# Pooled attention and a max-of-two feed-forward on one core: the first K load in two parts, and matmuls on a tile of ones at the start

## The chip, the core and the metric

The kernel runs on one core of one Trainium2 chip. The metric is the device time of one execution in microseconds; the number to compare is the median of several runs. Besides, one execution is recorded by the hardware profiler, and every duration below comes from that one.

The engines are named as in the profile: PE is TensorE's matmul and PEld its weight load, DVE is VectorE, ACT ScalarE, POOL GpSimd, SP SyncE. SPq is SP's queue of DMA issues.

## The reference

```python
def _attn_ref(q, k, v):                       # 8 x 8 heads, 1152 tokens, 64 wide
    scale = 1.0 / np.sqrt(D)
    q_pool = q.reshape(B, H, S // 2, 2, D).mean(axis=3)
    scores = scale * np.matmul(q_pool, k.transpose(0, 1, 3, 2))
    scores = scores - np.max(scores, axis=-1, keepdims=True)
    attn = np.exp(scores)
    attn = attn / (np.sum(attn, axis=-1, keepdims=True) + 1e-09)
    return np.matmul(attn, v).astype(np.float32)

def _moe_ref(x, w1, w2, w_out):               # x: 4608 x 512; w1, w2: 512 x 1024; w_out: 1024 x 512
    g = np.maximum(x @ w1, x @ w2)
    return (g @ w_out).astype(np.float32)
```

The heads' outputs, side by side, are the rows x. Inputs and output are float32.

## The kernel before, in words

**Pairs, groups, blocks.** Two heads of one batch are a pair; there are 32 pairs. For each pair, K (1152 x 64 for two heads) is loaded as kraw (128 partitions, 2 heads, 9 tiles of 64), cast to bf16 (kbf) and transposed to kT, 9 tiles of 128 columns. Q is loaded as qraw, two neighbouring rows are added (qp), and it is transposed to qpT (576 columns). The scores of a pair are a strip of 9 x 576 columns for each of the two heads; the strips of all pairs are laid end to end and cut into groups of 512 columns. For a group, PE computes both heads' scores into one of three PSUM tiles (sps0, sps1, sps2, in turn; line 548), and ACT takes the exponential of 128 x 1024 elements into et (line 555). When a pair's groups are done, PE multiplies et with V (lines 459 and 471), DVE normalizes (lines 481 to 491), and the result is transposed to xT. The feed-forward part follows, interleaved with later pairs.

**The beginning.** Pair 0 is handled in parts. Q comes in two loads (line 304), of 4 and 5 of 9 row groups: QA = 256 columns first, the other 320 later. Pair 0's strip is laid out accordingly: first all 9 tiles against the first 256 columns, then all 9 against the other 320. A group therefore has two K tiles at first: group 1 tiles 0 and 1, group 2 tiles 2 and 3, and so on; the fifth group has tile 8 with the first Q part and tile 0 with the second. K0 = (0, 2, 4, 9) cuts the first K's cast: tiles 0 to 1 and 2 to 3 by ACT (line 329), 4 to 8 by POOL (line 332). All three wait for the one load of kraw0 (line 296). PE transposes each part (line 428), DVE copies it to kT (line 435). Q's parts are added by DVE (line 346), transposed by PE (line 395), copied by DVE (line 402).

**What else runs early.** SP issues the loads in the order: first Q part, K0, second Q part, a quarter of w2 (line 626, into a free part of xT), Q1, K1, V0, and then more weights, Q, K and V. DVE turns each w2 quarter to bf16 (line 633) and each w_out quarter (line 637); PE transposes w2 (line 651), DVE copies (line 657); the product w2 with w_out is made later (line 667). POOL casts K1, K2, ... (line 320), adds Q2, Q3, ... (line 353), and casts V (line 359).

**Order.** The program builds a plan: each op names what it reads and writes, its engine and a cost; a planner emits ops by these modelled times. Then reorder() puts PE's and DVE's ops into an order written out by hand as strings. A letter of pe_order is the next op of that lane: "S" a score op, a digit an op that writes that PSUM bank. An op whose first written key begins with "s" is in lane S. In dve_order, "Q" is what belongs to no bank (the early adds), "W" the weight conversions, a digit the bank read. solve() puts in the semaphore waits; each engine runs its list strictly in order. On DVE the order at the start is: add of Q's first part, its copy, two kT copies, add of Q's second part, kT copy of tiles 4 to 8, conversion of w2's first quarter (633), copy of Q's second part (402).

## Time and profile before

| | us |
|---|---|
| median of 3 runs | 366.93 (366.34 to 367.17) |
| the profiled execution, its time | 366.77 |
| its span, first to last instruction | 365.1 |
| PE busy | 353.3 (97%), 5797 matmuls |
| ACT busy | 315.2 (86%) |
| DVE busy | 242.0 (66%) |
| POOL busy | 125.5 (34%) |
| DMA | 84.70 MB, mean 232 GB/s |

A row of the profile gives the line, the engine, the operation and the tiles (out<-in, without buffer numbers), how many, and then busy time, mean length and the idle time in front. A timeline row has start and length in us. Engines work side by side, so busy times don't add up to the span. A matmul's length includes its run through the array; neighbours overlap, so the pitch of a row of matmuls is shorter than the length of one.

### The profile page before, as it was taken

To read this page: it belongs to the slowest core of one execution; us is meant where nothing else is said; L and a number is where in the kernel's file an instruction comes from. 1 tells how busy PE (TensorE), PEld (TensorE's weight loads), DVE (VectorE), ACT (ScalarE), POOL (GpSimd) and SP (SyncE) were. 2 spreads that over 40 slices of the span, in tenths; PEclk is the share of its full clock that TensorE was granted. 3 is DMA by queue.
4 is the path that set the end of the run, shared out by engine and by line. 5 is a ranking of instruction groups with operands and counts; after the bars stand their busy time and mean duration, and the time that the engine had idled before them with its cause. 6 is when DMAs were issued, how large, how long until landed. Compare 5 with 4: busy or idle time off the path is not lost.

```text
span 365.1 us, 13058 instructions
## 1 busy us (share of the span) xinstructions
PE 353.3 (97%) x5797; PEld 217.3 (60%) x5797; DVE 242.0 (66%) x522; ACT 315.2 (86%) x356; POOL 125.5 (34%) x111
## 2 busy tenths in 40 slices
PE   3899999999999999999999999999999999999996
PEld 1466655665466656556666655656676664656563
DVE  3587478878688767785886955886778565533321
ACT  4999999999999999999999999999999999971221
POOL 1258984325453441461253421443434220000000
PEclk9899999999999999999999999999999999999999
DMA  7999997997999999997969999969999540422124
GB/s 284 407 394 399 397 297 247 239 275 210 287 324 254 272 294 327 265 341 196 322 137 232 254 264 306 239 144 262 343 283 198 75 107 20 75 18 59 41 76 115
DMA packets 77400, 84.70 MB, mean 232 GB/s; under 512 B 49952, under 2 KB 50208, under 8 KB 77344
## 3 DMA queue, kind: packets, MB, share of 16 engines
q1 hardware_dynamic: 76624, 82.82, 85.4%
q8 instruction: 45, 0.74, 0.9%
q10 hardware_dynamic: 720, 1.05, 0.8%
q14 instruction: 11, 0.09, 0.1%
HBM read 62.91 MB, written 9.44 MB: 198 GB/s over the span
## 4 chain that ended last, share of the span: by engine, by line
PE 93%; ACT 3%; DMA 1%; ACTq 1%; DVE 1%; issue 0%; SPq 0%; DVEq 0%
PE sps L548 22%; PE fb L789 13%; PE sps L459 11%; PE sps L756 10%; PE fb L459 10%; PE sps L789 7%; PE sps L822 5%; PE fb L756 5%; ACT et L555 3%; PE fb L667 2%; PE sps L471 2%; PE fb L471 2%; DMA kraw<-in_k_dram 1%; PE sps L729 1%; PE fb L428 1%; ACTq L693 1%
## 5 line engine op out<-in xcount | busy, mean ns | idle before, releaser
L555 ACT ACTIVATE et<-sps 128x1024 bf16<-128x1024 f32 (+1 forms) x336 | 306.4, 1006 | 15.5 <-PE sps L548 14.0
L548 PE MATMUL sps<-qpT,kT 64*128 64x256 bf16 (+7 forms) x1162 | 121.3, 288 | 1.4 <-ACT et L555 1.2
L413 DVE STREAM_TRANSPOSE qpT<-qp 32x288 bf16<-32x288 bf16 x216 | 101.4, 470 | 6.8 <-PE sps L548 2.4
L548 PEld LDWEIGHTS sps<-qpT,kT 64*128 64x128 bf16 x1162 | 46.8, 94 | 50.9 <-ACT et L555 16.4
L353 POOL TENSOR_TENSOR qp<-qraw 128x576 bf16<-128x576 f32 x30 | 42.2, 1406 | 76.3 <-DVE qpT L413 62.5
L359 POOL TENSOR_SCALAR vE<-vraw 128x1152 bf16<-128x1152 f32 x32 | 37.0, 1156 | 83.8 <-PE sps L459 52.0
L756 PE MATMUL sps<-xT,wd 64*128 64x512 bf16 (+3 forms) x448 | 52.6, 327 | 0.0
L789 PE MATMUL fb<-wo,stage 64*128 64x512 bf16 x288 | 43.5, 376 | 0.0
L459 PE MATMUL sps<-vE,et 128*128 128x65 bf16 x1224 | 43.4, 193 | 0.0
L765 DVE TENSOR_SCALAR stage<-sps 128x1024 bf16<-128x1024 f32 (+3 forms) x28 | 27.3, 974 | 23.6 <-PE sps L756 23.4
L459 PEld LDWEIGHTS sps<-vE,et 128*128 128x128 bf16 x1224 | 39.2, 97 | 5.9 <-issue 4.6
L459 PE MATMUL fb<-vE,et 128*128 128x65 bf16 x1080 | 39.4, 193 | 0.0
L459 PEld LDWEIGHTS fb<-vE,et 128*128 128x128 bf16 x1080 | 34.8, 97 | 7.5 <-issue 6.7
L320 POOL TENSOR_SCALAR kbf<-kraw 128x1152 bf16<-128x1152 f32 x31 | 35.7, 1151 | 9.5 <-DMA kraw<-in_k_dram 7.7
L756 PEld LDWEIGHTS sps<-xT,wd 64*128 64x128 bf16 x448 | 19.9, 94 | 14.7 <-DVE xT L615 1.2
L756 PE MATMUL fb<-xT,wd 64*128 64x512 bf16 (+3 forms) x192 | 23.2, 332 | 0.0
L789 PE MATMUL sps<-wo,stage 64*128 64x512 bf16 x160 | 23.2, 376 | 0.0
L789 PE MATMUL fb<-w,xT 64*128 64x512 bf16 x144 | 21.3, 376 | 0.0
L789 PEld LDWEIGHTS fb<-wo,stage 64*128 64x128 bf16 x288 | 13.4, 94 | 8.6
L765 DVE TENSOR_SCALAR stage<-fb 128x1024 bf16<-128x1024 f32 (+3 forms) x12 | 12.0, 1002 | 9.4 <-PE fb L756 9.2
L822 PE MATMUL sps<-wo,stage 128*128 128x512 bf16 (+2 forms) x64 | 15.7, 352 | 0.0
L481 DVE RECIPROCAL rc<-sps 128x5 f32<-128x5 f32 (+1 forms) x34 | 6.3, 187 | 14.0 <-PE sps L459 13.6
(71 smaller groups left out, 270.2 us busy)
## 6 DMA issues: line engine op xcount, KB each, us to landing
kraw<-in_k_dram SPq DMA_DIRECT2D x32, 576.0 KB, 7.1
vraw<-in_v_dram SPq DMA_DIRECT2D x32, 576.0 KB, 7.5
qraw<-in_q_dram SPq DMA_DIRECT2D x31, 576.0 KB, 5.8
out_dram<-stage SPq DMA_DIRECT2D x19, 256.0 KB, 7.3
out_dram<-stage SPq DMA_DIRECT2D x25, 128.0 KB, 3.3
xT<-in_moe_w_dram SPq DMA_DIRECT2D x4, 512.0 KB, 10.5
stage<-in_moe_w_out_dram SPq DMA_DIRECT2D x4, 512.0 KB, 13.9
stage<-in_moe_w_dram SPq DMA_DIRECT2D x4, 512.0 KB, 14.2
```

What stands on the lines that cost most here:

```text
L320: op("POOL", lambda g: g.tensor_scalar(kbf[s][:, :, :, :].rearrange("p t h d -> p h t d"), kraw[r][:, :, :, :], 1.0, 1.0, ALU.mult, ALU.mu ...
L353: op("POOL", lambda g: g.tensor_tensor(qpf[s][:, :, :], qraw[r][:, :, 0, :], qraw[r][:, :, 1, :], ALU.add), r=[f"qraw{r}"], w=[f"qp{s}.0", ...
L359: op("POOL", lambda g: g.tensor_scalar(vE[r][:, :, :, 0:D].rearrange("p t h d -> p h t d"), vraw[r][:, :, :, :], 1.0, 1.0, ALU.mult, ALU.m ...
L413: op("DVE", lambda e: e.transpose(view[dst:dst + 32, :, 32 * pb:32 * pb + 32], qpf[s][src:src + 32, :, 32 * db:32 * db + 32]), r=[f"qp{s}. ...
L459: last = e.matmul(fb[m][:, sb * 66:sb * 66 + 65], et[:, a:a + P], vE[vs][:, t, half, 0:65], start=(t == 0), stop=(t == NT - 1))
L471: last = e.matmul(fb[m][rows(half), NCH * 66:NCH * 66 + 65], et[:, a:a + NB], vE[vs][:, t, half, 0:65], start=(t == 0), stop=(t == NT - 1))
L548: last = e.matmul(sps[r][:, h, col:col + hi - lo], kT[i % 3][rows(h), t, :], qpT[i % 3][rows(h), lo:hi], start=True, stop=True)
L555: op("ACT", lambda e: e.activation(et2[:, :, c:c + z - a], sps[r][:, :, a - g * W:z - g * W], EXP, scale=scale), r=[f"s{r}"], w=keys + ([f ...
L756: last = e.matmul(fb[m + k][:, 0:size], wd[z, ct, (f0 + k) * P:(f0 + k + 1) * P], xT[z, ct, n0:n1], start=(turn == 0 and ct == 0), stop=(t ...
L765: dve(lambda e: e.tensor_scalar_max(gT[:, f0:f0 + 2, g0:g0 + size], wide[m // 2][:, :, 0:size], 0.0), [f"f{m}", f"f{m + 1}"], w + [f"f{m}" ...
L789: last = e.matmul(fb[m + k][:, :], lhs, rhs, start=(turn == 0 and j == 0), stop=(turn == 1 and j == NC_ + NF - 1))
L822: return e.matmul(fb[m][:, 0:c1 - c0], lhs, rhs[:, c0:c1], start=(j == 0), stop=(j == NC_ + NF - 1))
```

## The change

Three things are changed.

1. The first K is loaded in two DMAs: tiles 0 to 3 (256 KB, own semaphore d_k) and tiles 4 to 8 (320 KB). ACT's two casts wait for the first part, POOL's for the second. All later K loads are as before.
2. setup() has one more DVE op: a memset of a 128 x 128 tile of xnat[0] to 1.0. xnat[0] gets its own data later.
3. PE multiplies this tile with itself, into the first 128 columns of sps2: 24 times before Q's first transposes, 6 times between these and the first K transposes. Nobody reads the products. Each of the two is one op in lane S.

```diff
             op("POOL", ones, w=["vE0", "vE1", "vE2"])
+            op("DVE", lambda e: e.memset(xnat[0][:, 0, 0, :], 1.0), w=["warm"], cost=0.0)
+
+        def warm(n):
+
+            def go(e):
+                for j in range(n):
+                    last = e.matmul(sps[2][:, 0, 0:P], xnat[0][:, 0, 0, :], xnat[0][:, 0, 0, :],
+                                    start=True, stop=True)
+                return last
+            op("PE", go, r=["warm"], w=["s2"], cost=0.0)
 
-        def load_k(i):
+        def load_k(i, parts=((0, NT),)):
             b, h0, s = i // NHP, 2 * (i % NHP), i % 3
-            op("SP", lambda e: e.dma_start(
-                kraw[s][:, :, :, :].rearrange("p h t d -> p h (t d)"),
-                k[b, h0:h0 + 2, :, :].rearrange("h (p t) d -> p h (t d)", t=NT)),
-                w=[f"kraw{s}"], dma=f"d_k{s}", cost=1.54)
+            for lo, hi in parts:
+                op("SP", lambda e, lo=lo, hi=hi: e.dma_start(
+                    kraw[s][:, :, lo:hi, :].rearrange("p h t d -> p h (t d)"),
+                    k[b, h0:h0 + 2, :, :].rearrange("h (p t) d -> p h (t d)", t=NT)[
+                        :, :, lo * D:hi * D]),
+                    w=["kraw0.0"] if hi < NT else [f"kraw{s}"],
+                    dma="d_k" if hi < NT else f"d_k{s}", cost=0.0 if lo else 1.54)
...
             if hi < NT:
-                op("ACT", lambda e: e.activation(dst, src, COPY), r=["kraw0"], w=[f"kbf0.{lo}"],
+                op("ACT", lambda e: e.activation(dst, src, COPY), r=["kraw0.0"], w=[f"kbf0.{lo}"],
                    cost=(hi - lo) * 2 * D / 1200.0 + 0.03)
...
         K0 = (0, 2, 4, NT)
+        WARM = (24, 6)
         setup()
         load_q(0, ((0, Q0[1]),))
-        load_k(0)
+        load_k(0, ((0, K0[2]), (K0[2], NT)))
         load_q(0, ((Q0[1], QU),))
+        for n in WARM:
+            warm(n)
         cast_q0(0, 0, Q0[1])
...
         pe_order = (
-            "001S0SS0SS0SSSS00SSS1S01S11S00110SSS010S1S01SSS0010S11100SSS10S10S1S011SS000100S001SS0S11110SS00"
+            "S0S01S0SS0SS0SSSS00SSS1S01S11S00110SSS010S1S01SSS0010S11100SSS10S10S1S011SS000100S001SS0S11110SS"
...
         dve_order = (
-            "Q001Q0W00Q00W1W0W111100101W01WW10100010101W000100000110TTTTT0000TT100T0TTTT10TT0011TT060TTTTT0T0"
+            "QQ001Q0W00Q00W1W0W111100101W01WW10100010101W000100000110TTTTT0000TT100T0TTTT10TT0011TT060TTTTT0T"
```

The rest of the two strings is as before, moved along by the letters put in front. Apart from what is named here, every engine has the same instructions in the same order as before.

More of the change, by code (lines that the diff above doesn't have):

```diff
@@ L1365, in bass_funnel_attn__then__act_maxout2_kernel @@
         pe_order = (
-            "001S0SS0SS0SSSS00SSS1S01S11S00110SSS010S1S01SSS0010S11100SSS10S10S1S011SS000100S001SS0S11110SS00"
-            "000SS11011SSS101110S1S00001S1SS0010SS0111101SS111SS000001SS1116S666S6666S0000S000S0666S6S00S000S"
-            "1S111S66S6600S00S0006S0666S66S0101SS01001S666S666S6666S66S6666S6600S00S06S67666S0S777S000S06S006"
-            "6S660S6666S000S0066S660S66S6600S000S6666SS67777S000S06S6006S006S666S60S000S666S10S666S111S66S666"
-            "S06S0101S6S0101S666S666S6666S60S0000S666S0S6677S77S000S06S006666S666600S00666600S666060S006666S6"
@@ L1371, in bass_funnel_attn__then__act_maxout2_kernel @@
-            "66600S6666SS67777S0000S0606066S066S60060S0S00006S66S60S000S66S10S111S66S0000S0000S66S666S60S1001"
-            "S6S1001S66S666S6666S6666S666S600S000S6666SS67777S000S00S600S6666S66660S00S06666S066S60600S00S666"
-            "6SS67777S0S06666S6666S0000S6666SS76777S0000S6666S6666000S060S0066S6006S66600S06667SS77667S0000S0"
-            "00S000S006S666S60000SS01111S66S06000S000066S660S0600660S06600S666S6666S00S000S77776SS6666S000S00"
-            "066S66S066060S600S000S6666S66S660S0000S6766SS67677S0000S000S606S66S660S66S000S66S011S66S11S6666S"
@@ L1376, in bass_funnel_attn__then__act_maxout2_kernel @@
-            "60S001S6S1001S66S166S666S666S6666S00000S0S06666SS67777S00S0066660S66066S000S66660S66660S0006666S"
-            "06666S00S6676S66S0000S777S0000S6666S666600S00S6677SS67766S000S00S66660S6060S660S0000S6666S666600"
-            "S00S6666SS67777S000S6666S666S6000S000S66676SS6777S00000S0S6666S0666S6000S00S6666S0666S6000S00S67"
-            "676SS6767S0000S00S006S666S60S00001111S666S00S00000S0000S0S000000S0000006566672464337177321220363"
-            "513132621656031546236413516006744241576075656117433640600442521250362565640606060113162227254447"
@@ L1381, in bass_funnel_attn__then__act_maxout2_kernel @@
-            "377654521000032621513121073060040702323220407743336203300024222232234333334444444555555555555")
-        dve_order = (
-            "Q001Q0W00Q00W1W0W111100101W01WW10100010101W000100000110TTTTT0000TT100T0TTTT10TT0011TT060TTTTT0T0"
-            "0T101T6T0TTTTT00T1T0TTT0T1T6TTTTT6T66T77666TTTTTT6TT06T66677TTT0T6TT00TTT100T1TTTTTTT0001T0T16TT"
-            "TT66T6T776T66TT6T60TT666677T0TT60TTTT0000116TTT0TTTTTTT00TTT00T1T1666T6776TT6TT6TTTT6TTTTT666677"
-            "T06TTTT66667706TT6TTTTT66T7T7T66T0TTTTT000011T0T0TTT6T77TT6666T6TTTT6T0TT6766T67T0TT6TTT0TTTT100"
-            "0TT1T0T0T00TT116TTTTTT666677TT6TT6TT60TT66T6677T06TTTTTTT766667TT6T6TTTTT66667706TTTT766676T6TTT"
-            "6TT066667700000116066667706057316210724725")
+            "S0S01S0SS0SS0SSSS00SSS1S01S11S00110SSS010S1S01SSS0010S11100SSS10S10S1S011SS000100S001SS0S11110SS"
@@ new lines, in bass_funnel_attn__then__act_maxout2_kernel @@
+            "00000SS11011SSS101110S1S00001S1SS0010SS0111101SS111SS000001SS1116S666S6666S0000S000S0666S6S00S00"
+            "0S1S111S66S6600S00S0006S0666S66S0101SS01001S666S666S6666S66S6666S6600S00S06S67666S0S777S000S06S0"
+            "066S660S6666S000S0066S660S66S6600S000S6666SS67777S000S06S6006S006S666S60S000S666S10S666S111S66S6"
+            "66S06S0101S6S0101S666S666S6666S60S0000S666S0S6677S77S000S06S006666S666600S00666600S666060S006666"
+            "S666600S6666SS67777S0000S0606066S066S60060S0S00006S66S60S000S66S10S111S66S0000S0000S66S666S60S10"
@@ new lines, in bass_funnel_attn__then__act_maxout2_kernel @@
+            "01S6S1001S66S666S6666S6666S666S600S000S6666SS67777S000S00S600S6666S66660S00S06666S066S60600S00S6"
+            "666SS67777S0S06666S6666S0000S6666SS76777S0000S6666S6666000S060S0066S6006S66600S06667SS77667S0000"
+            "S000S000S006S666S60000SS01111S66S06000S000066S660S0600660S06600S666S6666S00S000S77776SS6666S000S"
+            "00066S66S066060S600S000S6666S66S660S0000S6766SS67677S0000S000S606S66S660S66S000S66S011S66S11S666"
+            "6S60S001S6S1001S66S166S666S666S6666S00000S0S06666SS67777S00S0066660S66066S000S66660S66660S000666"
@@ new lines, in bass_funnel_attn__then__act_maxout2_kernel @@
+            "6S06666S00S6676S66S0000S777S0000S6666S666600S00S6677SS67766S000S00S66660S6060S660S0000S6666S6666"
+            "00S00S6666SS67777S000S6666S666S6000S000S66676SS6777S00000S0S6666S0666S6000S00S6666S0666S6000S00S"
+            "67676SS6767S0000S00S006S666S60S00001111S666S00S00000S0000S0S000000S00000065666724643371773212203"
+            "635131326216560315462364135160067442415760756561174336406004425212503625656406060601131622272544"
+            "47377654521000032621513121073060040702323220407743336203300024222232234333334444444555555555555")
@@ new lines, in bass_funnel_attn__then__act_maxout2_kernel @@
+        dve_order = (
+            "QQ001Q0W00Q00W1W0W111100101W01WW10100010101W000100000110TTTTT0000TT100T0TTTT10TT0011TT060TTTTT0T"
+            "00T101T6T0TTTTT00T1T0TTT0T1T6TTTTT6T66T77666TTTTTT6TT06T66677TTT0T6TT00TTT100T1TTTTTTT0001T0T16T"
+            "TTT66T6T776T66TT6T60TT666677T0TT60TTTT0000116TTT0TTTTTTT00TTT00T1T1666T6776TT6TT6TTTT6TTTTT66667"
+            "7T06TTTT66667706TT6TTTTT66T7T7T66T0TTTTT000011T0T0TTT6T77TT6666T6TTTT6T0TT6766T67T0TT6TTT0TTTT10"
+            "00TT1T0T0T00TT116TTTTTT666677TT6TT6TT60TT66T6677T06TTTTTTT766667TT6T6TTTTT66667706TTTT766676T6TT"
+            "T6TT066667700000116066667706057316210724725")
```

## The prediction

> **What bounds the kernel now.** I read the chain of waits first (the page's part 4), then the same chain for the first microseconds, then the rows that the change touches, and last the TensorE clock in equal stretches.

> ```profile
> PE 93%; ACT 3%; DMA 1%; ACTq 1%; DVE 1%; issue 0%; SPq 0%; DVEq 0%
> ```

> TensorE (PE) sets the end. Its idle times, read from the view of waits, are 4.2 us for the first Q, 1.1 us for the first K cast, 0.6 us for L435, 1.2 us for L555, and under 1 us in all the rest of the span. From 14.45 us on its queue is practically never empty, so an earlier point in its fixed list is an earlier end, unless something later arrives at a fixed time. The chain at the start, in order of time (start, length, what):

> ```profile
> 1.25 3.90 DMA kraw<-in_k_dram
> ...
> 5.18 0.43 ACT kbf L329
> ...
> 5.74 0.39 PE fb L428 x2
> ...
> 6.15 0.30 DVE kT L435
> ...
> 6.50 0.61 PE sps L548 x4
> 7.11 0.65 PE fb L428 x5
> 7.76 0.56 PE sps L548 x3
> ...
> 8.34 4.70 ACT et L555 x5
> ```

> K's landing, two casts, transposes, copy and scores stand in a row before the first exp (7.15 us). From 8.34 us ScalarE (ACT) is continuous for 14 exps, to 21.32, and PE waits for it. Then the clock (columns: stretch, length, busy time of PE, PEld, DVE, ACT, POOL with counts, granted clock, DMA share, GB/s):

> ```profile
> 4.15:7.57 3.42, 2.11 (x21) 1.14 (x21) 1.22 (x4) 1.15 (x3) 0.73 (x1) 1.00 0.99 388
> 7.57:10.98 3.41, 3.37 (x35) 1.53 (x34) 1.92 (x3) 3.24 (x4) 0.00 (x0) 1.00 1.00 384
> 10.98:14.39 3.41, 1.97 (x29) 0.94 (x26) 2.18 (x3) 3.41 (x5) 2.43 (x2) 1.00 1.05 413
> 14.39:17.81 3.42, 3.34 (x39) 1.61 (x40) 2.09 (x5) 3.42 (x5) 0.00 (x0) 0.50 1.03 404
> ```

> The 1.00 of the first two rows is only the absence of a record: the rows of one shape say otherwise. Five L428 transposes take 0.72 us at 7.04 and 0.45 us at 13.41 (timeline: start, length, what; the other lines are used further down):

> ```profile
> 7.04 0.72 PE L428 MATMUL fb<-ident,kbf 128*128 128x128 bf16 x5
> ...
> 8.24 1.22 DVE L633 TENSOR_REDUCE xT<-xT 128x1024 bf16<-128x1024 f32 x1
> ...
> 9.29 1.09 PE L548 MATMUL sps<-qpT,kT 64*128 64x256 bf16 x8
> 9.39 0.32 DVE L402 COPY qpT<-fb 128x320 bf16<-128x320 bf16 x1
> ...
> 13.41 0.45 PE L428 MATMUL fb<-ident,kbf 128*128 128x128 bf16 x5
> ...
> 30.30 1.15 POOL L320 TENSOR_SCALAR kbf<-kraw 128x1152 bf16<-128x1152 f32 x1
> ...
> 32.76 0.45 PE L428 MATMUL fb<-ident,kbf 128*128 128x128 bf16 x5
> ```

> One matmul's own length is about 0.30 slow and 0.22 fast (L428's durations run 219 to 315 ns), so the pitch is (0.72-0.30)/4 = 0.105 us slow and (0.45-0.22)/4 = 0.057 fast. PE is thus at half clock until 10.98 us, at full clock for one stretch, at half again from 14.39 to 17.81, then full. A stretch 99% busy (7.57 to 10.98) was followed by full clock; one 62% busy (4.15 to 7.57) was not; one 58% busy at full clock was followed by half.

> **The change, step by step.** *K in two parts.* Q's first part lands at about 3.7 (issue 0.79, 2.9 to landing), K at 5.2 (1.25 plus 3.9): 1.5 us for 576 KB. The first 256 KB then land 320/576 of that earlier, 0.8 us: at 4.35. ACT's casts need only this part, so the first cast goes from 5.18 to 4.40, and PE's transposes, 0.56 us behind it, could go from 5.74 to 4.96.

> The split adds one DMA issue on SP, and all SP loads behind it (second Q part, the weights, K1, V0) are issued one issue, 0.42 to 0.47 us, later. The DMA engines are full from 2 us on (share 0.99 to 1.05), and loads further back land 6 to 8 us after issue, so the later issue is hidden by the queue ahead of it. Were that cover gone, every load would land up to 0.46 later. More, shorter pieces cost something: the 320 KB of Q's second part took 0.85 us, 2.66 ns per KB against K's 2.56, some 4% of K's 1.5 us, 0.06. I take 0.1 us for all later landings, bounds 0 and 0.46.

> The POOL cast of tiles 4 to 8 (L332, 5.24, 0.73 long) waits for the second part: 5.35 to 6.1, early enough for its transposes (7.04 before).

> *The memset on VectorE (DVE)* is not in the trace. GpSimd's memset of ident, same shape, takes 0.20; DVE's copy of 128x256 0.29; it is between 0.05 and 0.3. I take 0.2. DVE has nothing before 3.69 us, so Q's landing hides it.

> *The 24 ones-matmuls.* The engines begin at 0.78; memset and handover bring PE to about 1.1; 24 x 0.105 = 2.5 us; end 3.6, 3.9 with the last one's drain. Queued behind them are Q's transposes, which wait for L346's end until 4.17 anyway: cost 0, margin 0.3 us. *The 6 others* stand between Q's transposes (0.25 of streaming from 4.17) and K's: 6 x 0.105 = 0.63 slow, 0.34 fast. Slow, PE is free at 5.05 and K's transposes go at 5.05 instead of 4.96: cost 0.1; fast, 0. They write sps2, first wanted by the third score group, later on the same engine.

> *The first exps.* From K's transposes to the first exp the old rows take 7.15 - 5.74 = 1.41, of which 0.61 is scores (0.39 at 18.71, same shape, full clock). New first exp: 5.05 + 1.41 = 6.46 slow, 4.96 + 1.19 = 6.15 fast: 0.7 to 1.0 us earlier. The second group (0.17 of ACT idle at 8.34) then follows without a gap.

> *What holds the lead back: the fifth group.* It is the second half of the PE row at 9.29 (start about 9.77) and needs the second Q part in qpT, L402 at 9.39. On DVE that copy stands behind L633, which starts at 8.24, when its weights land (issue 2.22, 6.0 to landing = 8.22). This landing doesn't come earlier; with the 0.1 it is 8.32, and the group starts at 9.87. Its exp stood at 11.07 (7.15, then 8.34 and 0.91 apart). Full clock: 9.87 + 0.39 + 0.03 = 10.29, lead 0.78. Half clock: 9.87 + 0.64 = 10.51, lead 0.56; then L651 and the next group (1.4 us behind at half clock) bring 11.87 or so against an exp at 11.97, and the lead is 0.1, or 0.3 if full clock comes by 11.

> *The dense stretch.* The 3.4 us at half clock from 14.39 fell where PE was full: some 1.5 us of work. ACT ran out of scores for 0.58 us at 21.32. If that half-clock stretch goes or falls earlier, ACT gains up to 0.58 more: lead 1.36.

> *Cap.* K3's cast (POOL, 30.30 to 31.45) follows two landings that don't move, and its transposes stand at 32.76: 32.76 - 31.45 - 0.05 handover - 0.1 = 1.16 us is all PE can gain there. K4 gives the same (cast 36.22 to 37.37 after a DMA wait, transposes 38.71): 1.19.

> *Sum.* Lead 0.78 at the fifth group, 0.58 more at 21.32 if PE keeps full clock, cut to 1.16 by K3. Between 0.78 and 1.16 I take 1.0. The profiled run took 366.77 with a span of 365.1; 365.77 and a span of 364.1 follow. The median lies 0.16 above that run: 365.9.

> [...]

> **Rivals.**
> - *The clock isn't opened early.* The ones fill 2.5 us, then with Q's transposes and the six about 3.4 of the 4 us to 5.05, some 75 to 84% of any 3.41 us there: between the two rows above. Then only K's split acts: lead 0.1 to 0.3 at the sixth group, and part of the 0.58 may come back, since PE enters the dense stretch earlier. Gain 0.1 to 0.6, 366.3 to 366.8; about 366.55.
> - *Slower: a second half-clock stretch in dense work.* At full clock PE has less to do while ACT sets the pace (58% busy, then half clock, at 10.98 to 14.39). [...] In dense work half clock loses 1 - 0.057/0.105 = 0.46 us per us, 1.55 a stretch. The lead of 1.0 is gone from 2.2 us beyond the old 3.4 on. A whole second stretch gives 367.5 with that lead, and 368.4 if half clock at the sixth group has cut it to 0.1; about 368. Against: a dense stretch (from 14.39, 98%) was followed by full clock for good.
> - *More than the cap.* Should weights and K land earlier than I hold (the queue not full after all), 1.36 or more counts: 365.5 and below. The DMA share of 1.0 speaks against it.
> - *Hidden altogether.* A landing late by the full 0.46 puts the fifth group at 10.23 and its lead at 0.4; K3's cap at 0.8; about 366.5 to 366.9.

> **How the numbers follow.** Forecast 0.53, clock not opened 0.20, hidden 0.07, more than the cap 0.10, second stretch 0.10. The 0.2% that a measurement here can tell is 0.73 us: 366.2 and below is faster, 367.66 and above slower. The forecast's own width, 365.6 to 366.3, falls nearly all on the faster side; with "more" and a little of the first rival that is 0.60; same 0.31; slower 0.09, nearly all of the second stretch's. The runs before lie 0.6 below to 0.2 above their median. Range 365.3 to 367.1: below it some of "more", above it the second stretch; the bound of 0.46 lies inside.

> **What would show it.** First cast at 4.4, first exp at 6.2 to 6.5; no 0.17 gap before the second exp; PE pitch 0.057 at K's transposes; fifth group at about 9.9; no 0.58 gap near 20.5; K3's transposes right behind its cast. Wrong if five L428 transposes near 6 us still take 0.72, if Q's transposes start after 4.2, or if the granted clock is 0.5 for more than 3.4 us after 13.

## The result, and the profile after

| | before | after |
|---|---|---|
| median of 12 runs each, us | 366.84 (366.01 to 368.69) | 367.75 (366.67 to 368.71) |
| ratio, 95% interval | | 1.003 [1.0017, 1.0043] |
| profiled execution, us | 366.77, span 365.1 | 367.36, span 365.6 |
| mean granted clock in it | 0.995 | 0.991 |

The changed kernel is slower by 0.91 us, where the forecast, 365.9, was 1.0 below the 366.93 known then. The new lines are 13 further down: L342 and L345 are the casts of K by ACT and POOL, L441 K's transposes, L448 their copies to kT, L359 the adds of Q's parts, L561 the scores, L568 the exp, L646 the conversion of w2, L415 the copy of Q's transposes, L299 the ones.

First the page's shares of the chain of waits in after, which still say that TensorE sets the end:

```profile
PE 92%; ACT 2%; DMA 2%; DVE 1%; ACTq 1%; SPq 0%; issue 0%
```

The chain's beginning in after (start, length, what):

```profile
2.69 0.04 issue
2.73 6.25 DMA xT<-in_moe_w_dram
...
9.00 1.22 DVE xT L646
10.22 0.24 DVE qpT L415
...
10.51 0.61 PE sps L561 x3
```

Before, the chain ran through K's landing, its casts and the first exp, and ACT from 8.34 on. Now it runs through the landing of w2's first quarter, for 6.25 us. The timeline of after shows what became of the start (start, length, engine, what; in brackets the idle time in front and who ended it):

```profile
1.10 2.74 PE L299 MATMUL sps<-xnat 128*128 128x128 bf16 x24 [1.10 <-DVE xnat L293]
...
4.12 0.72 ACT L342 ACTIVATE kbf<-kraw 128x256 bf16<-128x256 f32 x2 [2.06 <-DMA kraw<-in_k_dram]
...
5.81 1.02 ACT L568 ACTIVATE et<-sps 128x1024 bf16<-128x1024 f32 x1 [0.97 <-PE sps L561]
6.35 0.73 POOL L345 TENSOR_SCALAR kbf<-kraw 128x640 bf16<-128x640 f32 x1 [4.80 <-DMA kraw<-in_k_dram]
...
7.14 0.45 PE L441 MATMUL fb<-ident,kbf 128*128 128x128 bf16 x5 [1.36 <-POOL kbf L345]
...
7.52 0.47 PE L561 MATMUL sps<-qpT,kT 64*128 64x256 bf16 x4
7.66 0.49 DVE L359 TENSOR_TENSOR qp<-qraw 128x320 bf16<-128x320 f32 x1 [2.14 <-DMA qraw<-in_q_dram]
8.03 1.02 ACT L568 ACTIVATE et<-sps 128x1024 bf16<-128x1024 f32 x1 [1.19 <-PE sps L561]
8.07 0.48 DVE L448 COPY kT<-fb 128x640 bf16<-128x640 bf16 x1
...
8.61 0.61 PE L561 MATMUL sps<-qpT,kT 64*128 64x256 bf16 x4 [0.62 <-DVE kT L448]
9.00 1.22 DVE L646 TENSOR_REDUCE xT<-xT 128x1024 bf16<-128x1024 f32 x1 [0.45 <-DMA xT<-in_moe_w_dram]
...
9.26 2.92 ACT L568 ACTIVATE et<-sps 128x1024 bf16<-128x1024 f32 x3 [0.21 <-PE sps L561]
...
10.51 0.61 PE L561 MATMUL sps<-qpT,kT 64*128 64x256 bf16 x4 [0.34 <-DVE qpT L415]
...
12.67 1.02 ACT L568 ACTIVATE et<-sps 128x1024 bf16<-128x1024 f32 x1 [0.48 <-PE sps L561]
```

The first cast is 1.06 us earlier than before (4.12 against 5.18) and the first exp 1.34 (5.81 against 7.15). Then POOL's cast waits for K's second part until 6.35 (5.24 before), PE waits 1.36 us for that cast, and ACT has 1.19 us without scores ahead of the second exp: in PE's list the transposes of tiles 4 to 8 stand ahead of the second group's scores, so this group needs all of K. The third group's scores wait 0.62 us for the kT copy L448, which stands on DVE behind the add L359, and that add starts when Q's second part has landed (7.64). The third exp starts at 9.26, where before it stood at 9.25 (8.34 plus 0.91): two exps later the lead is gone. The fifth group starts at 10.51 (9.77), because the copy L415 stands behind L646, whose weights landed at 8.98 (8.22).

The loads of the first 3.1 us tell why. Of before, then of after (tiles, how many, KB, us from issue to landing):

```profile
kraw<-in_k_dram SPq DMA_DIRECT2D x1, 576.0 KB, 3.9
...
xT<-in_moe_w_dram SPq DMA_DIRECT2D x1, 512.0 KB, 6.0
qraw<-in_q_dram SPq DMA_DIRECT2D x1, 320.0 KB, 4.3
```

```profile
xT<-in_moe_w_dram SPq DMA_DIRECT2D x1, 512.0 KB, 6.2
kraw<-in_k_dram SPq DMA_DIRECT2D x1, 320.0 KB, 4.6
qraw<-in_q_dram SPq DMA_DIRECT2D x1, 320.0 KB, 5.4
...
kraw<-in_k_dram SPq DMA_DIRECT2D x1, 256.0 KB, 2.9
```

With the issue times (1.25; 1.71, 2.22, 2.73) K is complete at 6.27 (5.16 before), Q's second part lands at 7.64 (5.99), the w2 quarter at 8.98 (8.22). The issues moved by at most 0.51 us, the landings by 0.76 to 1.65.

Last the clock of after, in stretches cut at the changes of the granted clock (columns as in the prediction):

```profile
0.89:4.30 3.41, 3.15 (x33) 2.82 (x34) 0.58 (x2) 1.35 (x2) 0.58 (x5) 1.00 0.68 218
4.30:7.72 3.42, 1.86 (x25) 1.03 (x23) 0.84 (x4) 1.57 (x3) 0.73 (x1) 1.00 1.00 346
7.72:11.13 3.41, 2.44 (x28) 0.82 (x24) 2.29 (x4) 2.89 (x3) 0.00 (x0) 0.50 1.00 375
11.13:14.54 3.41, 3.14 (x31) 1.91 (x32) 1.58 (x2) 2.93 (x5) 2.25 (x2) 0.50 1.05 411
14.54:17.96 3.42, 2.59 (x47) 1.41 (x45) 2.51 (x5) 3.42 (x5) 0.18 (x1) 1.00 1.02 403
```

The ones filled 92% of the first stretch, and the second ran at full clock: five L441 transposes take 0.45 us at 7.14, not 0.72. But in it PE was busy only 54% (it waited for POOL's cast and for kT), and two stretches at half clock follow. Two of the expectations below call a change of the granted clock from half to full the opening of the gate, and the way back its closing.

For after and for all executions of the experiments, before's there included, the mean granted clock is listed with the time. One stretch of 3.41 us at half clock takes 0.5 x 3.41 / 365 = 0.0047 off the mean, so 0.991 is two such stretches, 0.986 three, and 0.998 or more is called a whole clock below. Half clock ahead of the first record doesn't count (before's profiled execution has 0.995, which is its stretch from 14.39 alone, though its pitch at 7.04 was 0.105 us too), so an execution in which full clock comes late, but then stays, is listed as whole too (e1's profiled one: full from 14.73, listed with 1.0). Of before's executions in the four comparisons of the experiments, 87 of 104 had a whole clock, with a median of 366.27; the other 17 had 367.22. The profiled execution of before, with its half-clock stretch at 14.39, is thus of the kind that is rarer in these comparisons. Of after's 12 executions one had a whole clock (367.88), one a mean of 0.995, six 0.990 or 0.991, and four 0.986.

### The profile page after: what moved, and what is told of

It is laid out like the page before. It is cut to its first block, busy times and chain, and to the rows that moved or that the text cites. A ratio compares the mean times of both kernels' runs of the same rounds, so it can differ in the third digit from the quotient of the medians.

```text
span 365.6 us, 13120 instructions
## 1 busy us (share of the span) xinstructions
PE 356.0 (97%) x5827; PEld 220.1 (60%) x5827; DVE 242.1 (66%) x523; ACT 315.5 (86%) x356; POOL 125.4 (34%) x111
## 3 DMA queue, kind: packets, MB, share of 16 engines
q10 hardware_dynamic: 720, 1.05, 0.8%
## 4 chain that ended last, share of the span: by engine, by line
PE 92%; ACT 2%; DMA 2%; DVE 1%; ACTq 1%; SPq 0%; issue 0%
PE sps L561 21%; PE fb L802 13%; PE sps L472 11%; PE sps L769 10%; PE fb L472 10%; PE sps L802 7%; PE sps L835 5%; PE fb L769 5%; PE fb L680 2%; PE sps L484 2%; DMA xT<-in_moe_w_dram 2%; PE fb L484 2%; ACT et L568 2%; PE sps L742 1%; ACTq L706 1%; PE fb L742 1%
## 5 line engine op out<-in xcount | busy, mean ns | idle before, releaser
L568 ACT ACTIVATE et<-sps 128x1024 bf16<-128x1024 f32 (+1 forms) x336 | 306.7, 1004 | 16.8 <-PE sps L561 15.0
L561 PE MATMUL sps<-qpT,kT 64*128 64x256 bf16 (+7 forms) x1162 | 121.0, 287 | 1.9 <-DVE kT L448 0.8
L561 PEld LDWEIGHTS sps<-qpT,kT 64*128 64x128 bf16 x1162 | 47.0, 94 | 51.0 <-ACT et L568 15.3
```

Of the source, the lines that this page charges most:

```text
L561: last = e.matmul(sps[r][:, h, col:col + hi - lo], kT[i % 3][rows(h), t, :], qpT[i % 3][rows(h), lo:hi], start=True, stop=True)
L568: op("ACT", lambda e: e.activation(et2[:, :, c:c + z - a], sps[r][:, :, a - g * W:z - g * W], EXP, scale=scale), r=[f"s{r}"], w=keys + ([f ...
```

## The experiments

"Ratio" is against before on the same chip. "K, Q, w2" are the landings in the profiled execution, issue plus time to landing: all of the first K, Q's second part, w2's first quarter. Before has 5.16, 5.99, 8.22. "512-exp" is the start of the first exp over 128x512 elements, the same instruction in all kernels, at 45.59 in before's profile; the span beside it shows whether the distance stays.

| label | median (range) | before | ratio [95%] | K, Q, w2 | 512-exp, span | whole clock |
|---|---|---|---|---|---|---|
| after | 367.75 (366.67 to 368.71) | 366.84 | 1.003 [1.0017, 1.0043] | 6.27, 7.64, 8.98 | 45.65, 365.6 | 1 of 12 |
| e1_split_only | 367.09 (366.38 to 368.54) | 366.34 | 1.0025 [1.0013, 1.0036] | 6.76, 7.71, 8.97 | 45.62, 365.1 | 11 of 12 |
| e2_warm_only | 366.57 (365.6 to 368.93) | 366.34 | 1.0007 [0.999, 1.0024] | 5.29, 6.23, 7.58 | 45.12, 364.5 | 4 of 12 |
| e3_split_heads | 367.69 (366.66 to 369.13) | 366.34 | 1.003 [1.0017, 1.0043] | 5.97, 7.17, 8.45 | 45.76, 365.2 | 8 of 12 |
| e4_after_swap | 368.88 (366.9 to 369.89) | 366.34 | 1.0047 [1.0026, 1.0067] | 6.20, 7.86, 9.15 | 48.35, 367.9 | 2 of 12 |
| e5_warm_fill | 366.83 (365.68 to 369.29) | 366.27 | 1.0012 [0.9993, 1.0031] | 5.22, 6.21, 7.75 | 44.46, 364.5 | 11 of 12 |
| e6_split_fill | 368.38 (367.19 to 370.45) | 366.27 | 1.0061 [1.0037, 1.0085] | 6.72, 7.66, 8.92 | 45.72, 366.0 | 4 of 6 |
| e7_split_act | 367.24 (366.52 to 367.95) | 366.27 | 1.0021 [1.001, 1.0032] | 5.54, 6.35, 8.32 | 45.37, 364.9 | 6 of 12 |
| e8_q_extra | 366.70 (366.12 to 368.29) | 366.27 | 1.0017 [1.0005, 1.0029] | 5.35, 6.39, 7.87 | 46.23, 366.2 | 8 of 12 |
| e9_split_far | 368.14 (367.77 to 369.61) | 366.34 | 1.005 [1.0034, 1.0066] | 7.71, 6.42, 8.98 | 46.48, 366.0 | 3 of 6 |
| e10_q_first_two | 367.54 (366.92 to 368.49) | 366.34 | 1.0028 [1.0017, 1.0038] | 5.85, 6.67, 7.95 | 46.59, 366.0 | 7 of 11 |
| e11_warm_fill4 | 368.01 (366.54 to 371.67) | 366.34 | 1.0045 [1.0023, 1.0067] | 5.25, 6.50, 8.07 | 47.08, 369.9 | 11 of 12 |
| e12_split_behind_q | 367.15 (366.25 to 368.82) | 366.28 | 1.0026 [1.0013, 1.004] | 6.12, 4.51 (all of Q), 7.93 | 45.07, 364.5 | 7 of 12 |

In the kernels with the first K and Q loaded as before (before, e2, e5, e11) the landings lie at 5.16 to 5.29, 5.99 to 6.50 and 7.58 to 8.22; that is the spread against which a late landing is read. Each kernel has one trace.

**e1_split_only and e2_warm_only: each half of the change alone.** e1 keeps the two loads and has neither memset nor ones; e2 keeps the ones and loads K as before.

```diff
# e1_split_only, against after
-            op("DVE", lambda e: e.memset(xnat[0][:, 0, 0, :], 1.0), w=["warm"], cost=0.0)
...
-        WARM = (24, 6)
+        WARM = ()
# e2_warm_only, against after
-        load_k(0, ((0, K0[2]), (K0[2], NT)))
+        load_k(0)
```

> K in two parts, no tile of ones and no matmuls on it. Theory A (the split's shorter pieces slow the loads: in the changed kernel's trace w2's first quarter lands at 8.98 instead of 8.22 us, and every later load some 0.75 late): w2's quarter lands near 8.9 here too, the fifth group starts near 10.4, and the time is at or above that of the changed kernel, 0.5 to 1.0 us above before, since half clock lasts as before. Rival B (the ones-matmuls are what costs, by the clock or by the loads that they disturb): w2's quarter lands at 8.2 to 8.4, first exp near 6.4, time equal to before or up to 0.6 below.

> K in one load as before, with the tile of ones and the 24 and 6 matmuls. Theory A: loads land as before (w2's quarter near 8.2), PE's first transposes run at full clock in most executions, the time is 0 to 0.8 us below before. Rival B: the time is 0.5 to 1.0 us above before, like the changed kernel, with the half-clock stretches moved or the loads late although K comes in one piece.

e1 costs 0.75 us at the median, e2 0.23 with an interval that holds 1; the sum, 0.98, is near the 0.91 of both together. The late landings are all there in e1, without a single matmul of ones. Its timeline:

```profile
4.36 0.72 ACT L341 ACTIVATE kbf<-kraw 128x256 bf16<-128x256 f32 x2 [2.29 <-DMA kraw<-in_k_dram]
...
6.84 0.73 POOL L344 TENSOR_SCALAR kbf<-kraw 128x640 bf16<-128x640 f32 x1 [5.28 <-DMA kraw<-in_k_dram]
...
9.00 1.22 DVE L645 TENSOR_REDUCE xT<-xT 128x1024 bf16<-128x1024 f32 x1
```

So the split by itself makes most of the loss, and it needs no meeting with the ones. That e1's profiled span equals before's (365.1) is no contradiction: e1's full clock came at 14.73 and stayed, while before's half-clock stretch from 14.39 fell into dense work. The whole-clock executions, 366.27 of before against 367.09 (e1's median, 11 of 12 whole), give 0.82. e2 misses its first expectation in part: the loads are in time, but in the profile K's first transposes still run at half clock (four in 0.61 us) and the time isn't below before's. In e2 the ones don't make the clock whole; 8 of its 12 executions have a half-clock stretch after the first full clock, where before has 17 of 104.

**e3_split_heads: K0 in two loads, one per head.** Pieces of 2304 bytes, as before, where the change's have 1024 and 1280; the casts wait for both loads, so nothing is gained early.

```diff
-        load_k(0)
+        for h in range(2):
+            op("SP", lambda e, h=h: e.dma_start(
+                kraw[0][:, h:h + 1, :, :].rearrange("p h t d -> p h (t d)"),
...
```

> The kernel before, with the first K loaded by two DMAs of one head each: one issue more, but the pieces stay 2304 bytes; the casts wait for both. No ones. If the length of the pieces is what delays the loads, w2's quarter lands within 0.15 us of 8.22 and the time is that of before (within 0.3). If the additional DMA as such delays them, it lands near 8.9 and the time is 0.5 to 1.0 us above before.

K lands 0.81 late, Q's second part 1.18, of which 0.46 and 0.47 are the later issue; w2 lands at 8.45, 0.23 past the spread and between the two expectations. The ratio is 1.003, and the casts, which wait for all of K here, make the first exp 0.82 later. So pieces of the old length don't prevent late landings of K and Q. Whether shorter pieces add to it (w2 at 8.97 in e1) can't be told from one trace of each.

**e4_after_swap: after, with the copy of Q's second part ahead of the w2 conversion on DVE.** The fifth group then no longer waits for the late weights.

```diff
-            "QQ001Q0W00Q00W1W0W111100101W01WW10100010101W000100000110TTTTT0000TT100T0TTTT10TT0011TT060TTTTT0T"
+            "QQ001Q00W0Q00W1W0W111100101W01WW10100010101W000100000110TTTTT0000TT100T0TTTT10TT0011TT060TTTTT0T"
```

> The changed kernel with one letter pair of the DVE order exchanged: the copy of Q's second part now stands ahead of the conversion of w2's first quarter, so the fifth group no longer waits for that landing. If the fifth group's wait is what took the lead: it starts near 9.9 instead of 10.5, the 0.48 us of ScalarE idle at 12.2 shrinks to 0.2 or less, and the time falls by 0.2 to 0.6 against the changed kernel. If K1 and Q1, also late, bind just as much, the time stays within 0.2.

A miss: 368.88. The copy did come ahead (9.89), but in the profiled execution the stretch at full clock was 43% busy, and four at half clock follow (to 22.35):

```profile
5.28:8.69 3.41, 1.48 (x18) 0.64 (x15) 1.29 (x4) 1.83 (x2) 0.73 (x1) 1.00 1.01 330
8.69:12.10 3.41, 2.74 (x29) 1.44 (x30) 1.54 (x3) 2.83 (x4) 0.00 (x0) 0.50 1.03 402
...
18.90:22.35 3.45, 3.45 (x52) 2.45 (x48) 3.22 (x4) 2.95 (x4) 2.56 (x2) 0.50 1.04 396
```

ACT is busy only 2.8 to 3.0 us in each of these, for want of scores, and the 512-exp is at 48.35. The wait for the weights wasn't taken away either, it moved: the conversion now runs from 10.13 (9.00 in after), and PE's transposes of w2 (L664), which stand ahead of the sixth group's scores, wait for it.

```profile
10.13 1.21 DVE L646 TENSOR_REDUCE xT<-xT 128x1024 bf16<-128x1024 f32 x1
...
11.40 1.04 PE L664 MATMUL fb<-ident,xT 128*128 128x128 bf16 x8 [0.52 <-DVE xT L646]
```

The sixth exp starts at 13.02 (12.67 in after). How much of the 12 executions' median the half-clock stretches make is open: five with a mean clock of 0.98 took 368.8 to 369.9 and five with 0.986 or 0.991 took 366.9 to 367.9, but the two listed as whole took 368.95 and 369.05, and when full clock came first in those isn't recorded.

**e5_warm_fill and e6_split_fill: more ones, so that full clock stays.** WARM is (27, 12), and six times five ones stand between the next score groups; e5 with K in one load, e6 with K in two.

```diff
-        WARM = (24, 6)
+        WARM = (27, 12)
+        FILL = (5, 5, 5, 5, 5, 5)
...
-            "S0S01S0SS0SS0SSSS00SSS1S01S11S00110SSS010S1S01SSS0010S11100SSS10S10S1S011SS000100S001SS0S11110SS"
+            "S0S01S0SSF0SSF0SFSFSFSF00SSS1S01S11S00110SSS010S1S01SSS0010S11100SSS10S10S1S011SS000100S001SS0S11110SS"
```

> K in one load; 27 and 12 ones-matmuls at the start, and six times 5 more between the score groups 3 to 9, into a part of the second fb bank that nobody reads then. Theory G (the gate closes again after the ones because PE has too little to do at full clock while ScalarE sets the pace; a 3.41 us stretch under about 60% busy closes it, one over about 90% opens it): the granted clock has no 0.5 record after its first 1.0 in nearly all executions (mean clock 0.999 to 1.0), and the time falls by 0.5 to 1.0 us against K in one load with 24 and 6 ones (366.57), to 365.6 to 366.0. Rival: closings are as frequent as there (8 of 12 executions below 0.998), or the time stays at 366.3 to 367 although the clock is whole, because loads and ScalarE hold the lead anyway.

> The changed kernel with the same additional ones-matmuls between the groups. If the changed kernel's loss is the sum of late loads and closings, the closings go (clock 0.999 to 1.0), and the late loads stay: 366.6 to 367.1, 0.6 to 1.1 us below the changed kernel and some 0.7 above the same kernel with K in one load. If the loads alone are the loss, the time stays within 0.3 of the changed kernel.

In e5 the clock did what the prediction wanted. Its stretches:

```profile
1.71:5.12 3.41, 3.41 (x38) 3.15 (x37) 0.72 (x2) 0.36 (x1) 0.00 (x0) 1.00 0.93 309
5.12:8.54 3.42, 2.80 (x36) 1.46 (x33) 2.17 (x5) 2.37 (x4) 0.73 (x1) 1.00 1.02 387
8.54:11.95 3.41, 3.31 (x55) 2.07 (x55) 2.09 (x4) 3.41 (x5) 1.15 (x1) 1.00 1.05 410
```

Full clock from 5.12 on (the mean granted clock is 0.999), no stretch of the five from 1.71 to 18.78 under 76% busy, 11 of 12 executions whole. The 60 and 90% of theory G are an estimate: in before and after half clock followed shares of 54 and 58%, full clock followed 92 and 99%. As thresholds the runs don't bear them out (half clock stayed after 98% in e1 and 94% in e2, full clock after 52% in e6). The 512-exp is at 44.46, 1.13 earlier than in before's profile, which is the lead that the prediction wanted at its upper end. The time is still no better than before's (1.0012, the interval holds 1). About half of the lead is no lead against a before at whole clock (span 364.6 in those of its executions that took 366.29 and 366.30, 365.1 in the profiled one). The rest, 0.66 us, went between 142 and 152 us, where PE waits for nothing that the profile shows; the last section comes back to this. The profiled execution took 366.27; why the median is 0.56 higher no trace shows. e6 missed both of its expectations: with K in two, the same ones give 368.38, 1.55 above e5 and 0.63 above after. Its profile has the late landings again (6.72, 7.66, 8.92); it lags by 0.13 us at the 512-exp, and another 0.8 goes at 145 and 153 us, in waits like e5's.

**e7_split_act: the second part of K issued by ACT's queue.**

```diff
# against e1
-                op("SP", lambda e, lo=lo, hi=hi: e.dma_start(
+                op("ACT" if lo else "SP", lambda e, lo=lo, hi=hi: e.dma_start(
```

> K in two parts without ones, the second part issued from ScalarE's queue instead of SP's, so SP's later loads are issued when they were before. If SP's additional issue of 0.46 us delays the loads: w2's first quarter lands at 7.6 to 8.3, and the time is 0.5 to 0.8 us below K in two parts from SP (367.09). If the additional transfer itself makes DMA engines stall (packets of 0.7 to 2.1 us between 3.8 and 7.2 us, which all four kernels with K in two loads show and the two with K in one don't): it lands at 8.5 to 9.1, with such packets, and the time stays within 0.4 of 367.09.

Q's second part lands at 6.35 and w2 at 8.32, nearly as before; the DMA engines move 393 GB/s between 3.25 and 5.25 us, as much as before (396), and no packet there takes over 0.54 us. So one more transfer, by itself, doesn't make the later loads late. But the two parts now run side by side, and the first part, the one that was to be early, lands 4.3 us after its issue, at 5.54; Q's first part, too, is later (4.01 against 3.67). The time doesn't fall as the first expectation wanted: the ratio is 1.0021, and in the profile the first exps are 0.38 us later than before's.

**e8_q_extra and e9_split_far: one more load elsewhere, and the two parts of K apart.** e8 is before with Q's second part in two loads, behind K. e9 is e1 with the order Q first part, K first part, Q second part, K second part.

```diff
# e8_q_extra, against before
-        load_q(0, ((Q0[1], QU),))
+        op("SP", lambda e: e.dma_start(
+            qraw[0][:, 4:6, :, :].rearrange("p u r d -> p (u r d)"),
...
+        load_q(0, ((6, QU),))
# e9_split_far, against e1, in reorder()
+        sp[2], sp[3] = sp[3], sp[2]
```

> The kernel before, with Q's second part in two loads (tiles 4 to 5 and 6 to 8): one DMA more in the same stretch, but K untouched and no ones. If any additional early load delays those behind it: w2's first quarter lands at 8.4 to 9.1 with packets over 0.7 us, and the time is 0.4 to 0.9 above before. If it is K's split that matters (its casts, its pieces): landing at 7.6 to 8.3, time within 0.2 of before.

> K in two parts, no ones, but Q's second part is loaded between K's two parts (order: Q first part, K first part, Q second part, K second part). In the five traces with K's parts back to back on SP, K is whole at 5.97 to 6.76 us and w2's first quarter lands at 8.45 to 9.15; with K in one load at 5.16 to 5.35 and 7.58 to 8.22. If two loads of K next to each other are what stalls the DMA engines, w2's quarter lands at 7.6 to 8.3 here and the time falls below K in two parts (367.09) by 0.3 to 0.7. If a second short load directly behind the first short one is enough, whichever it is, landing stays at 8.4 to 9.1 and the time at 367 or above.

e8: K at 5.35, just past the spread, Q's second part and w2 within it, 1.0017. One early DMA more, behind a whole K, is not what costs 0.8 to 1.7 us. e9: K complete at 7.71, w2 at 8.98 as in after, 1.005; putting another load between the two parts doesn't mend it, and the second part of K, which the second group needs, now comes behind Q's second part.

**e10_q_first_two and e12_split_behind_q: short loads at the front, with and without K.** e10 is before with Q's first part in two loads of 128 KB and K in one. e12 is e1 with all of Q in one load of 576 KB ahead of K's two parts.

```diff
# e10_q_first_two, against before
-                    qraw[s][:, lo:hi, :, :].rearrange("p u r d -> p (u r d)"),
+                    qraw[s][:, lo:hi if hi == QU else 2, :, :].rearrange("p u r d -> p (u r d)"),
...
+        more = op("SP", lambda e: e.dma_start(
+            qraw[0][:, 2:4, :, :].rearrange("p u r d -> p (u r d)"),
...
# e12_split_behind_q, against e1
-                    qraw[s][:, lo:hi, :, :].rearrange("p u r d -> p (u r d)"),
+                    qraw[s][:, lo:QU, :, :].rearrange("p u r d -> p (u r d)"),
```

> The kernel before with Q's first part in two loads of 128 KB (K in one, no ones): one short load more at the very front. If short loads at the front, before the queue behind them is full, are what makes engines stall: K is whole at 5.9 or later, w2's quarter lands at 8.4 to 9.1, packets over 0.7 us appear between 3.5 and 7.2, and the time is 0.5 to 1.0 above before. If it is peculiar to K's split: K at 5.2 to 5.5, w2's quarter at 7.6 to 8.3, time within 0.3 of before.

> All of Q in one load of 576 KB first, then K in its two parts, then as before (as many loads as before, no ones). If short loads behind one another at the very front are what makes the engines stall, Q's 1.4 us of transfer cover the two short K loads here: K is whole at 5.9 to 6.2 (its place in the queue), w2's first quarter lands at 7.6 to 8.3 without packets over 0.7 us behind K, and the time is 0.1 to 0.5 above before, for the first exp later. If two loads of K next to each other stall wherever they stand, w2's quarter lands at 8.4 or later and the time is 0.5 to 1.2 above before.

In e10 K is whole and lands 0.69 late, Q's second part 0.68; 0.46 and 0.47 of this are the later issue. The first cast shows it:

```profile
5.87 0.72 ACT L331 ACTIVATE kbf<-kraw 128x256 bf16<-128x256 f32 x2 [3.80 <-DMA kraw<-in_k_dram]
```

The DMA engines move only 50 GB/s between 3.0 and 3.5 us there (301 in before), and seven packets that start at 2.87 to 3.06 take 0.75 to 0.9 us. But w2 lands at 7.95, within the spread. So e10 fits neither expectation: the short loads do cost a stretch at a low rate with K whole, and it has passed by the time of w2. The time is 0.95 above before's in the whole-clock executions (367.27 against 366.32), and the first exp is 0.69 later.

In e12 K is split as in e1, with as many bytes and as many loads ahead of w2 as before:

```profile
5.28 0.72 ACT L346 ACTIVATE kbf<-kraw 128x256 bf16<-128x256 f32 x2 [3.22 <-DMA kraw<-in_k_dram]
...
6.20 0.73 POOL L349 TENSOR_SCALAR kbf<-kraw 128x640 bf16<-128x640 f32 x1 [4.65 <-DMA kraw<-in_k_dram]
```

The w2 quarter lands at 7.93 there, within the spread, and not at 8.97 as in e1. So the split as such doesn't make w2 late: behind one long load it doesn't, behind a short one it does (e1, e9). That the short load in front is the reason isn't shown beyond this, for e12 also has one load fewer than e1, and e10, with short loads and a whole K, has w2 in time. The time of e12 is 0.87 above before's at the median and 0.34 in the whole-clock executions (366.61 against 366.27). K's first part, behind all of Q, is ready no earlier than K was before (5.28 against 5.18), and the first exp is 0.11 later; the rest is open.

**e11_warm_fill4: e5 with fewer ones,** WARM = (25, 8) and fills of four, to see whether the loss at 142 us in e5 hangs on the number of matmuls.

> K in one load with 25 and 8 ones at the start and six times 4 between the groups (57 in all; e5 had 69). In e5's trace PE led the kernel before by 1.13 us up to the 130th exp and lost 0.66 of it at 142.9 and 150.6 us, in waits that no engine ends, 128 matmuls apart. If these waits hang on where in the list of instructions the program stands (an instruction block that comes late), 12 matmuls less move or remove them, and the time is 0.2 to 0.7 below e5 (366.83). If the lead is lost anyway, the time is within 0.2 of e5. Clock: whole in nearly all executions if 4 between groups are enough to keep the gate open, as in e5.

It became slower, not faster: 368.01, with a range up to 371.67. The profiled execution is the slowest of the twelve; the last section shows it.

## Why the prediction was wrong

**The step that failed** is "I take 0.1 us for all later landings, bounds 0 and 0.46", in the step on K in two parts. Measured: 1.11 us for the whole of K, 1.65 for Q's second part, 0.76 for the w2 quarter; e1 has 1.60, 1.72 and 0.75. The argument was that a full queue hides a later issue. Its reading of the trace was too generous: the share of 0.99 to 1.05 stands in the rows from 4.15 us on, and from 2 to 4 us before has 0.87. And where the share was high in after, the engines moved less. Two quarters of a microsecond, of before and then of after (columns as above; the last two are DMA share and GB/s):

```profile
4.25:4.50 0.25, 0.25 (x8) 0.21 (x8) 0.00 (x0) 0.00 (x0) 0.00 (x0) 1.00 1.05 416
4.50:4.75 0.25, 0.10 (x4) 0.00 (x0) 0.11 (x1) 0.00 (x0) 0.00 (x0) 1.00 1.08 378
```

```profile
4.25:4.50 0.25, 0.25 (x9) 0.25 (x6) 0.14 (x1) 0.25 (x2) 0.00 (x0) 1.00 0.95 297
4.50:4.75 0.25, 0.25 (x6) 0.14 (x4) 0.15 (x1) 0.25 (x2) 0.00 (x0) 1.00 1.04 271
```

From 3.25 to 5.25 us after has a share of 0.98 and 323 GB/s, before 1.03 and 396, e1 0.91 and 252. The share of busy time didn't show that a busy engine was delivering less. In this time single packets on single engines take 0.9 and 2.1 us in after (starts at 4.07 and 5.49), four of 0.73 to 1.0 in e1, up to 1.5 in e3; before and e2 have none over 0.7 there. Such packets alone don't make loads late, though: e5 and e11, with K whole and landings within the spread, have some of up to 1.0 and 1.1. Why the rate falls is open: no row of the trace shows what those packets wait for.

**Two steps leaned on this one.** "Early enough for its transposes (7.04 before)" held POOL's cast of tiles 4 to 8 against the old place of these transposes. With the lead they would have stood 0.7 to 0.8 us earlier, at about 6.3, so the predicted end at 6.1 left little to spare; the cast ended at 7.08. And "the second group then follows without a gap" became a gap of 1.19 us. The fifth group, which the prediction took for the one that holds the lead back, came too late to matter: the second and third group had used it up.

**The first steps held.** First cast 4.12 (predicted 4.40), first exp 5.81 (6.15 at full clock), the memset 0.17 (0.2) and hidden, the 24 ones over by 3.84, Q's transposes at 3.90, before the 4.17 that they waited for. The cost of these parts on the path was nothing, as forecast.

**Full clock came early, and did not stay.** The stretch ahead of it was 92% busy, between the 62% and the 99% of the prediction's rows. The pitch at K's transposes is (0.45 - 0.22) / 4 = 0.057. What the slower rival (chance 0.10) feared came in its place: the next stretch was 54% busy and two half-clock stretches followed; 11 of the 12 executions have at least one, four of them three. The rival's price, about 368, is near the measured 367.75, but partly by luck: e1, with full clock only from 14.73, shows that late loads, which the rival doesn't have, make most of the loss. In the profile the stretch was thin mostly for the late K: 1.36 us of PE's idle time in it are the wait for POOL's cast. In after's trace full clock came at 4.30, behind 2.74 us of ones (from 1.10) and Q's transposes (from 3.90). But e2, whose ones fell over two stretches, 49% and 75% busy, stayed at half clock until 13.03. Stretches of 54% (after), 58% (before) and 43% (e4) were followed by half clock. The share alone is no sharp rule either way: stretches at half clock of 94% (e2, e8) and 98% (e1) weren't followed by full clock, and at full clock one of 52% (e6, with the late K) and some of 62 to 66% (e7, e9, e12) kept it. What else decides isn't shown.

**The fifth group** started at 10.51, not at 9.87, and its exp had no lead (the third to fifth exp start at 9.26 plus 0.97 each, so the fifth near 11.2; before 11.07). The cap at K3, 1.16, was never reached.

**The 0.58 us of the dense stretch** came back in the profiled pair: after lags by 0.70 us at the sixth exp and by 0.06 at the sixteenth, the one behind before's gap of 0.58, since its half-clock stretches lay earlier and ACT ran from 12.67 to 30.39 without a gap. But in most executions it wasn't there to be had: 87 of 104 of before in the later comparisons have no such half-clock stretch. The prediction read this term off one execution, 366.77, and moved the sum to the median by 0.16; against the whole-clock median of 366.27 nothing of it is left. (How many of the result's own 12, with their median of 366.84, had the stretch isn't recorded.)

**That a lead or lag at the dense stretch reaches the end** held: the distance at the 512-exp is the distance of the spans within 0.15 us in e1, e2, e3, e4, e7, e9, e10 and e12. The exceptions are after (0.06 against 0.5), e5, e6, e8 and e11, and these five are the ones with waits of the kind in the last section.

Taken together: the 1.3 us of lead at the first exp is used up by the third, and the split costs 0.75 us without any ones (e1 against its own before). After loses 0.91 against its own, so 0.16 is left for the ones; the medians themselves lie 0.66 apart, but so do, by 0.50, the medians of before in the two comparisons (366.34 and 366.84). After's executions go with their half-clock stretches (those with 0.991 have a median of 367.22, those with 0.986 one of 368.14), but not sharply: its one execution with a whole clock took 367.88. That the ones win nothing even where all loads are in time is e2's 1.0007. None of the versions tried is faster than before.

## What to carry to other kernels

A load split so that its head comes earlier must be judged by the landings of everything behind it; a DMA share near 1.0 didn't say that nothing can be lost there (from 3.25 to 5.25 us 0.98 went with 323 GB/s in after, 1.03 with 396 in before), and here K in two short loads behind a short one made what followed land 0.2 to 1.7 us late (after, e1, e3). Full clock that came early didn't last in after and e4, where the next stretch was 54% and 43% busy; in e5, with 82%, it did: look for the first thin stretch behind the warm-up before counting on full clock. A part that is to be early helps only as far as the next instruction in a fixed list that needs the rest (the second group's scores here: 1.19 us without scores on ACT). Before a gain is read off a profiled execution, see whether the other executions have what is to be removed, by their mean granted clock.

## What had not been expected

PE at times waits for nothing that the profile shows, and at the same places in its list. The timeline of PE in e11, where this costs most:

```profile
31.99 0.25 PE L401 MATMUL fb<-ident,qp 64*64 64x64 bf16 x5 [1.11 <-issue]
...
74.10 0.38 PE L570 MATMUL sps<-qpT,kT 64*128 64x256 bf16 x3 [1.44 <-issue]
...
156.00 0.27 PE L481 MATMUL fb<-vE,et 128*128 128x65 bf16 x3 [0.68 <-issue]
```
